# A windowed-attention and MLP kernel: two tensors of the first four chunks loaded in runs of four tokens, and fifty operations with ranks of their own

## The chip, the cores and the metric

The kernel runs on one core of a Trainium2 chip. The time is the device time of one execution in microseconds (us): 217.26 as the median of three runs before the change (217.12 to 218.15). The trace comes from one profiled execution, which took 217.13 us; its span, from the first to the last recorded instruction, is 215.5 us.

The core has TensorE (PE, matmuls; its weight loads are shown apart as PEld), VectorE (DVE), ScalarE (ACT), GpSimd (POOL) and SyncE (SP). SP, ACT and POOL also issue transfers to 16 DMA engines; POOL's transfers can change the type (f32 to bf16) on the way.

## What is computed

Attention over 4 batches, 8 heads, 768 tokens and 64 dimensions, in which a token sees the 4 first tokens and the last 128 up to itself; then a layer norm and an MLP with residual over 512 features:

```python
scores = scale * np.matmul(q, k.transpose(0, 1, 3, 2))
keep = is_sink | in_window
scores = np.where(keep, scores, -1000000000.0)
a = np.exp(scores - np.max(scores, axis=-1, keepdims=True))
a = a / (np.sum(a, axis=-1, keepdims=True) + 1e-09)
attn_out = np.matmul(a, v)
...
x = attn_out.transpose(0, 2, 1, 3).reshape(B, S, H * D)
xn = (x - mu) / np.sqrt(var + 1e-06) * g_ln
out = x + np.maximum(xn @ w_ch1, 0.0) @ w_ch2
```

Inputs and output are float32; the matmuls run in bf16.

## The kernel before

The 3072 tokens are 24 tiles of 128; two tiles make a chunk, three chunks a batch, so there are 12 chunks, each with one MLP of 256 tokens.

For scores the kernel needs q and k with the dimensions on the partitions (kT and qT: four pairs of heads, 128 rows for a pair, 256 tokens). It gets them in three ways. Chunk 0 is loaded in f32 by SP (k) and ACT (q), two loads each for four heads (L666, into natf), cast to bf16 (L670, natc), transposed by matmuls against an identity (L678) and evicted from PSUM into kT and qT (L649). Chunks 1 to 3 are loaded and cast by POOL (L584, into natp), transposed on PE (L597 for chunk 1, one tensor at a time; L604 for chunks 2 and 3, k and q together) and evicted. Chunks 4 to 11 are transposed by the DMA engines. In chunks 0 to 3 a row of the staging tile holds two neighbouring tokens of a head, 512 bytes in the input; the eviction puts the tokens back in order.

Tiles 0 to 3 are attended one by one (`attend_tile`): the mask is added by matmuls (L750) for tiles 0 to 2 and applied on DVE (L780) for tile 3; scores on PE (L770 for tiles 0 and 1, L729 after), exp on ACT (L777), and for tiles 2 and 3 scores against the first four tokens (L785, exp L788). The values (L852, L857) are followed by the reciprocal and the scaling (L870, L872) and by `normalise`: statistics, aggregate and subtraction of the mean on DVE (L880, L882, L884), the power on POOL (L889, L890). For tiles 0 to 3 the result xc is transposed on PE (L897) and evicted with g_ln into xnt (L908). From chunk 2 on the DMA engines do this transpose, and w1 is scaled by g_ln once instead (L1108, L1109), after the MLPs of chunks 0 and 1 have used it unscaled.

The MLP of chunk 0 works by single tiles (L1038), the others by 256 tokens (L1045); relu is on ACT (L1055) or DVE (L1057), the second layer is L1074 and its end L1082. Where PE has a gap in the first 24 us, matmuls on constants fill it (L1146).

Nothing of this is issued in the order of the source. Every step is an operation of a planner (`Plan.op`) with the engines it may run on, a cost, a rank (`prio`, smaller is earlier) and the buffers it needs. `Plan.run` lays them out once, when the program is built, and takes among the operations that could start at about the same time the one of the smallest rank:

```python
t0 = min(c[0] for c in cand[e])
st, o, took = min((c for c in cand[e] if c[0] <= t0 + self.WINDOW[e]), key=lambda c: (c[1].prio, c[1].seq))
```

The result is one fixed list for each engine, carried out in order: an instruction that waits holds up everything behind it on its engine. Costs of transfers are constants such as `SW_P` (L217) and `HW_F` (L219); they decide the order alone. POOL's transfers are served in the order of issue and use eight semaphores in turn, so POOL waits before it issues a ninth until the first has landed.

Of the kernel before, what the change touches and what calls it, by code (L numbers as in the profile page):

```python
# [65 lines left out]
class Plan:  # L66
# [9 lines left out]
    def __init__(self):  # L76
        self.ops = []
        self.rings = {}

# [3 lines left out]
    def op(self, name, engs, prio, emit, reads=(), writes=(), rw=(), dma=None, after=(), mode="n", hold=(), nb=0.0):  # L83
        o = Op()
        o.name, o.engs, o.prio, o.emit, o.dma = name, engs, prio, emit, dma
# [125 lines left out]
def fix(occ, extra=0.09):  # L211
# [5 lines left out]
SW_P = (1.47, 0.7, 0.9)  # L217
SW_W = (2.65, 0.7, 0.9)
HW_F = (0.8, 2.2, 0.5)  # L219
# [13 lines left out]
           w1p=(1.6, 2.6, 2.7, 2.8), pm=3, w2p=(4.5, 4.51, 4.52, 4.53), apart=2, vs0=(2.0, 13.0), by_tile=1, vp=(0.0, 0.1, 2.0, 2.1, 4.55, 4.56), ld1=0.05, t0=0.8, warm=5.6, pm0=-40.0, w1g=17.0, gtt=1.25)  # L233

# [134 lines left out]
def kernel(  # L369
# [42 lines left out]
    ring("natf", 2, [128, H, 2, 64], FP32)  # L412
    ring("natc", 4, [128, 2, 4, 64], BF16)
    ring("nat", 8, [128, H, 64], BF16)
    ring("natp", 4, [128, H, 2, 64], BF16)
    ring("vn", 7, [128, H, 65], BF16)
    ring("kT", 4, [128, HP, 256], BF16)
    ring("qT", 3, [128, HP, 256], BF16)
# [159 lines left out]
    def by_pairs(c, what, d):  # L578
        b, R = c // RC, c % RC
        nats, pts, whole = [], [], len(what) == 1  # L580
        for nm, src, T, ld in what:
            nat = Buf(f"{nm}n{c}", "natp")
            ap = src[b, :, 256 * R:256 * R + 256, :].rearrange("h (p i) d -> p h (i d)", i=2)
            P.op(f"{nm}ld{c}", {"POOL": (0.9, 0.93)}, ld, lambda e, nat=nat, ap=ap: G.dma_start(  # L584
                nat.t.rearrange("p h i d -> p h (i d)"), ap), writes=[nat], dma=SW_P)
            nats.append(nat)
            pts.append([Buf(f"pt{nm}{c}", "pair")] if len(what) > 1 else [Buf(f"pt{nm}{2 * c + r}", "one") for r in range(2)])

        def half(pt, r):
            return (pt[0].t[:, r, :] if len(pt) == 1 else pt[r].t).rearrange("p (h i m) -> p h i m", h=HP, i=2)  # L590

        def tr(e):
            for nat, pt in zip(nats, pts):
                for hp in range(HP):
                    for i in range(2):
                        for h2 in range(2) if whole else ():
                            nc.tensor.matmul(pt[hp // 2].t[64 * h2:64 * h2 + 64, 256 * (hp % 2) + 128 * i:256 * (hp % 2) + 128 * i + 128],  # L597
                                             lhsT=nat.t[:, 2 * hp + h2, i, :], rhs=ident, start=True, stop=True, skip_group_check=True)
                        if whole:
                            continue  # L600
                        for h2 in range(2):
                            for r in range(2):
                                rs, cs = slice(64 * r, 64 * r + 64), slice(64 * h2, 64 * h2 + 64)
                                nc.tensor.matmul(half(pt, r)[cs, hp, i, :], lhsT=nat.t[rs, 2 * hp + h2, i, :],  # L604
                                                 rhs=ident[rs, rs], start=True, stop=True, skip_group_check=True)
        o = P.op(f"tr{what[0][0]}{c}", pe(0.45 if whole else 0.28 * len(what)), d, tr, reads=nats + [Bc["ident"]], hold=[w[2] for w in what],
                 writes=[x for pt in pts for x in pt], mode="h" if whole else "q")
        for (nm, src, T, ld), pt in zip(what, pts):
            for r in range(2):
                t, done = 2 * c + r, Buf(f"{nm}T{2 * c + r}")  # L610
                if c == 1:
                    trs[t] = [o]
                evict(f"ev{nm}{t}", d + 0.05 + 0.02 * r, 512,
                      lambda pt=pt, r=r: pt[r].t.rearrange("p (h i m) -> p h m i", h=2, i=2) if whole else
# [575 lines left out]
```

## Time and profile before

| | us |
|---|---|
| median of three runs | 217.26 |
| the profiled execution | 217.13 |
| its span | 215.5 |
| PE busy | 207.7 |
| DVE, ACT, POOL busy | 114.7, 110.0, 111.4 |
| matmuls of the MLPs: L1074, L1045, L1038 busy | 87.4, 79.3, 8.1 |

The profile shows when each instruction ran and what ended the wait before it. The chain of waits follows the last instruction back to what released it, step by step. A line number stands for the kernel's line, an arrow for what is written from what; buffer numbers are left out. The DMA engines are at 0.9 or more of their time in nearly every slice up to about 160 us.

### The profile page before, as it was taken

The numbers are of one execution on the slowest core, as the hardware profiler recorded it, in microseconds if no ns is written. First come the engines' busy times: TensorE is split into PE (matmuls) and PEld (weight loads), VectorE is DVE, ScalarE is ACT, GpSimd is POOL, SyncE is SP. The second block draws the span as 40 slices with busy tenths as digits, with TensorE's granted clock in tenths as the row PEclk, the third lists the DMA queues.
The fourth block names the chain that finished last, engine by engine and source line by source line (L and its number), as shares of the span: only waits on it lengthen the run. The fifth ranks groups of instructions, "written<-read, shape, count | busy, mean of one in ns | idle before, by whom it ended". The sixth has DMA issues, their size and how long they took to land.

```text
span 215.5 us, 6681 instructions
## 1 busy us (share of the span) xinstructions
PE 207.7 (96%) x2766; PEld 144.2 (67%) x2766; DVE 114.7 (53%) x315; ACT 110.0 (51%) x178; POOL 111.4 (52%) x166
## 2 busy tenths in 40 slices
PE   6799999999999999999999999999999999999992
PEld 2567975755865865865865865865865865866862
DVE  5689875698355356356355356356265365353011
ACT  4796497395662562562652652652652652621600
POOL 7978542499871980971971980971970120110000
PEclk9999999999999999999999999999999999999999
DMA  5999999999999999899899899896899202202102
GB/s 155 189 189 208 191 207 192 185 150 146 167 188 180 110 139 137 90 177 143 117 110 177 117 147 144 109 157 127 117 119 162 75 3 76 73 3 81 41 20 93
DMA packets 104557, 28.07 MB, mean 130 GB/s; under 512 B 94788, under 2 KB 101576, under 8 KB 104520
## 3 DMA queue, kind: packets, MB, share of 16 engines
q0 software_dynamic: 69872, 13.18, 92.2%
q1 hardware_dynamic: 33592, 13.87, 35.2%
q10 hardware_dynamic: 1056, 0.52, 0.9%
q8 instruction: 23, 0.38, 0.8%
q14 instruction: 14, 0.11, 0.2%
HBM read 27.43 MB, written 6.29 MB: 156 GB/s over the span
## 4 chain that ended last, share of the span: by engine, by line
PE 89%; DVE 5%; DMA 2%; ACT 1%; issue 1%; SPq 0%; DVEq 0%
PE one L1074 40%; PE one L1045 36%; PE pair L979 3%; DMA natf<-in_k_dram 2%; PE one L952 2%; PE one L959 2%; PE one L968 1%; DVE st L880 1%; DVE xnt L908 1%; PE one L987 1%; PE one L1038 1%; DVE x L872 1%; PE pair L604 1%; PE pair L729 1%; DVE pe L780 1%
## 5 line engine op out<-in xcount | busy, mean ns | idle before, releaser
L1074 PE MATMUL one<-w,h 128*128 128x512 bf16 (+1 forms) x400 | 87.4, 371 | 0.0
L1055 ACT ACTIVATE h<-one 128x512 bf16<-128x512 f32 x93 | 55.6, 598 | 46.9 <-PE one L1045 42.6
L1045 PE MATMUL one<-xnt,w 128*128 128x256 bf16 x704 | 79.3, 273 | 0.0
L1045 PEld LDWEIGHTS <-w 128*128 128x128 bf16 x704 | 68.6, 98 | 10.4
L1074 PEld LDWEIGHTS <-h 128*128 128x128 bf16 x400 | 37.3, 98 | 39.6
L997 ACT ACTIVATE pe<-pair 128x768 bf16<-128x768 f32 x36 | 27.2, 810 | 41.0 <-PE pair L979 41.0
L644 POOL DMA_DIRECT2D vn<-in_v_dram x59 | 38.7, 694 | 11.4 <-DMA w<-in_moe_w_ch_dram 6.8
L889 POOL TENSOR_SCALAR st<-st 128x1 f32<-128x1 f32 x24 | 8.5, 355 | 61.8 <-DVE st L882 61.2
L1020 DVE RECIPROCAL rec<-one 128x4 f32<-128x4 f32 x36 | 6.4, 178 | 62.9 <-PE one L968 51.4
L1082 DVE SCALAR_TENSOR_TENSOR ot<-one,st,x 128x512 f32<-128x512 f32 (+1 forms) x25 | 18.2, 728 | 13.9 <-PE one L1074 9.0
L890 POOL TENSOR_TENSOR st<-st,mhalf 128x1 f32<-128x1 f32 x24 | 16.7, 696 | 2.0
L880 DVE BATCH_NORM_STATS2 st<-x 128x6 f32<-128x512 bf16 x24 | 16.7, 695 | 0.8
L1022 DVE TENSOR_TENSOR x<-one,rec 128x256 bf16<-128x256 f32 x36 | 15.3, 425 | 1.2
L702 POOL DMA_DIRECT2D nat<-in_k_dram x16 | 15.0, 938 | 1.6 <-DMA natp<-in_q_dram 1.0
L702 POOL DMA_DIRECT2D nat<-in_q_dram x16 | 14.3, 905 | 0.0
L1002 DVE TENSOR_TENSOR pe<-pe,band 128x768 bf16<-128x768 bf16 x24 | 12.2, 551 | 0.0
L979 PE MATMUL pair<-qT,kT 64*64 64x128 bf16 (+1 forms) x528 | 9.2, 204 | 0.0
L884 DVE TENSOR_SCALAR xc<-x,st 128x512 bf16<-128x512 bf16 x24 | 8.5, 353 | 0.9
L952 PEld LDWEIGHTS <-pe 128*128 128x128 bf16 (+1 forms) x144 | 6.2, 97 | 2.9 <-issue 0.8
L1038 PE MATMUL one<-xnt,w 128*128 128x128 bf16 x128 | 8.1, 219 | 0.0
L777 ACT ACTIVATE pe<-pair 128x1024 bf16<-128x1024 f32 (+1 forms) x8 | 7.1, 916 | 1.8 <-PE pair L729 1.4
L979 PEld LDWEIGHTS <-kT 64*64 64x64 bf16 x528 | 7.2, 108 | 0.4 <-ACT w L1109 0.4
(110 smaller groups left out, 165.1 us busy)
## 6 DMA issues: line engine op xcount, KB each, us to landing
out_dram<-ot SPq DMA_DIRECT2D x23, 256.0 KB
w<-in_moe_w_ch_dram POOLq DMA_DIRECT2D x8, 512.0 KB, 14.8
nat<-in_k_dram POOLq DMA_DIRECT2D x16, 128.0 KB, 4.5
nat<-in_q_dram POOLq DMA_DIRECT2D x16, 128.0 KB, 5.3
vn<-in_v_dram POOLq DMA_DIRECT2D x44, 32.0 KB, 5.9
vn<-in_v_dram POOLq DMA_DIRECT2D x15, 64.0 KB, 6.1
natp<-in_k_dram POOLq DMA_DIRECT2D x3, 256.0 KB, 14.7
vn<-in_v_dram POOLq DMA_DIRECT2D x6, 128.0 KB, 9.3
```

The lines of the kernel that those rows point to most:

```text
L644: P.op(f"vld{t}_{i}", {"POOL": (0.8, 0.85)}, prio + 0.001 * i, lambda e, p0=p0, n=n, hs=hs, src=src: G.dma_start(m.t[p0:p0 + n, hs, 0:64], ...
L702: lambda e, nat=nat, ap=ap: G.dma_start(nat.t, ap), writes=[nat], dma=SW, after=gate(c))
L880: P.op(f"bn{t}", {"DVE": fix(0.60)}, d + 0.12, lambda e: V.bn_stats(st.t[:, 8:14], x.t), reads=[x], writes=[st, mv])
L890: G.tensor_tensor(st.t[:, 16:17], st.t[:, 17:18], mhalf, op=ALU.pow)),
L979: nc.tensor.matmul(pps[u].t[64 * g:64 * g + 64, h2, col + c0:col + c0 + n], lhsT=kt.t[rs, hp, k0:k0 + 64], rhs=qT.t[rs, hp, q0:q0 + n], st ...
L997: nc.scalar.activation(pes[j].t.rearrange("p a b -> p (a b)")[:, 0:768].rearrange("p (a b) -> p a b", a=2), pps[j].t[:, :, 0:384], AF.Exp, ...
L1002: V.tensor_mul(at_s, at_s, band[j] if r > 1 else edge[r][j].unsqueeze(1).to_broadcast([128, 4, 192]))
L1022: P.op(f"x{t - 1}{u}", {"DVE": dve(256)}, d + 0.051 + 0.002 * u, lambda e, u=u, rc=rc, pv=pv: V.tensor_tensor(x.t[:, 256 * u:256 * u + 256 ...
L1045: nc.tensor.matmul(ph.t[:, 256 * s:256 * s + 256], lhsT=w1[ht // 4][:, j, 128 * (ht % 4):128 * (ht % 4 + 1)], rhs=xnt.t[:, j, :], start=j ...
L1055: nc.scalar.activation(hb.t, ph.t, AF.Relu)
L1074: nc.tensor.matmul(pc.t[:, 0:wd], lhsT=(h1[2 * s + i].t[:, 128 * ii:128 * ii + 128] if by_tile else h1[ht // 2].t[:, 256 * (ht % 2) + 128 ...
L1082: V.scalar_tensor_tensor(ot.t[:, sl], in0=pc.t[:, 0:wd], scalar=st.t[:, 16:17], in1=x.t[:, sl], op0=ALU.mult, op1=ALU.add),
```

## The change

Chunks 0 to 3 are loaded in runs of four tokens, 1 KB of the input, instead of two. A staging row holds four tokens of a head, and 64 rows hold the 256 tokens of a chunk; the other 64 rows hold other heads (chunks 1 to 3) or the other tensor (chunk 0). Each load of chunks 1 to 3 becomes two, for four heads and 64 partitions each (`by_fours` instead of `by_pairs`). In chunk 0 one staging tile holds k (rows 0 to 63) and q (rows 64 to 127) of the same four heads; each cast and transpose then makes k and q of one pair of heads at once, and kT and qT of chunk 0 lie in one tile `kq0`. The number of transposing matmuls and evictions stays.

A table `NUDGE` adds to the ranks of 50 operations: the new order was found by a search. Two cost constants of the planner follow the new loads. The scaling of w1 waits for the last use of each of its two halves per part instead of the last one in the source's order.

```diff
     def op(self, name, engs, prio, emit, reads=(), writes=(), rw=(), dma=None, after=(), mode="n", hold=(), nb=0.0):
         o = Op()
+        n = self.named[name] = self.named.get(name, -1) + 1
+        prio += NUDGE.get(f"{name}#{n}" if n else name, 0.0)
...
-SW_P = (1.47, 0.7, 0.9)
+SW_P = (0.67, 0.7, 0.9)
...
-HW_F = (0.8, 2.2, 0.5)
+HW_F = (0.7, 2.2, 0.5)
...
+NUDGE = {
+    "ones0": 42.7, "w1ld1": 0.5, "w2ld0": 1.4, "w2ld2": 9.4, "w2ld3": 12.6, "kld0": 12.3, "evf0": 11.2, "cast2": 16.2, "vld0": -14.7,
+    "vld1": -4.6, "x00": 17.1, "x01": 126.8, "ag0": 64.6, "evx0": 9.4, "sc1_0": -11.3, "rc11": -11.1, "trk1": -3, "sc2_0": -89.5,
+    "pm21": -8.8, "bn2": 46.3, "ag2": 5.7, "xc2": 32.2, "trx2": 17.1, "sc3_1": -91, "mk3_1": -6.3, "sk3": -9.1, "x30": 21, "xc3": 78.7,
+    "trx3": 69, "vld4": 5.5, "sc21": -16.1, "xc4": 6.1, "bn5": 21.8, "rs5": 21.5, "kld30": -6.8, "kld31": 11, "qld31": -10.4, "evq7": -6.2,
+    "vld6_0": -13.3, "vld6_1": -3.5, "vld6_3": -1.7, "vld7_0": 33, "vld8_0": -12.1, "vld8_1": -8.7, "vld9_0": 70.9, "vld9_2": -8.9,
+    "kld50": 7.4, "vld10_0": 7.7, "o10": 43.1, "pc40_1": -1.8}
...
-    ring("natf", 2, [128, H, 2, 64], FP32)
-    ring("natc", 4, [128, 2, 4, 64], BF16)
+    ring("natf", 2, [128, 4, 4, 64], FP32)
+    ring("natc", 4, [128, 4, 2, 64], BF16)
...
-    ring("natp", 4, [128, H, 2, 64], BF16)
+    ring("natp", 4, [128, 4, 4, 64], BF16)
...
+    kq0 = consts.tile([128, 2, HP, 256], BF16, name="kq0")
...
-    def by_pairs(c, what, d):
+    def by_fours(c, what, d):
...
-            ap = src[b, :, 256 * R:256 * R + 256, :].rearrange("h (p i) d -> p h (i d)", i=2)
-            P.op(f"{nm}ld{c}", {"POOL": (0.9, 0.93)}, ld, lambda e, nat=nat, ap=ap: G.dma_start(
-                nat.t.rearrange("p h i d -> p h (i d)"), ap), writes=[nat], dma=SW_P)
+            for hh in range(2):
+                ap = src[b, 4 * hh:4 * hh + 4, 256 * R:256 * R + 256, :].rearrange("h (g i) d -> g h (i d)", i=4)
+                P.op(f"{nm}ld{c}{hh}", {"POOL": (0.6, 0.63)}, ld + 0.001 * hh, lambda e, nat=nat, ap=ap, hh=hh: G.dma_start(
+                    nat.t[64 * hh:64 * hh + 64].rearrange("p h i d -> p h (i d)"), ap), writes=[nat], dma=SW_P)
...
+                            for hh in range(2):
+                                rs = slice(64 * hh, 64 * hh + 64)
+                                nc.tensor.matmul(half(pt, hh)[64 * h2:64 * h2 + 64, h1, i, :], lhsT=nat.t[rs, 2 * h1 + h2, i, :],
                                                  rhs=ident[rs, rs], start=True, stop=True, skip_group_check=True)
...
                 for hh in range(2):
-                    hs = slice(4 * hh, 4 * hh + 4)
-                    for i, (x, T) in enumerate(((k, kT_b[c]), (q, qT_b[c]))):
-                        nm, src, part = "kq"[i], nats[i], Buf(f"{'kq'[i]}l{hh}")
-                        ap = x[b, hs, 0:256, :].rearrange("h (p i) d -> p h (i d)", i=2)
+                    src, part, done = Buf(f"f{hh}", "natf"), Buf(f"fl{hh}"), Buf(f"kqT{hh}")
+                    for w, x in enumerate((k, q)):
+                        ap = x[b, 4 * hh:4 * hh + 4, 0:256, :].rearrange("h (g i) d -> g h (i d)", i=4)
+                        P.op(f"{'kq'[w]}ld{hh}", {("SP", "ACT")[w]: (0.53, 0.53)}, -70 + hh,
+                             lambda e, src=src, ap=ap, w=w: (nc.sync if e == "SP" else nc.scalar).dma_start(
+                                 src.t[64 * w:64 * w + 64].rearrange("p h i d -> p h (i d)"), ap), writes=[src, part], dma=HW_F)
+                    for h1 in range(2):
+                        u = 2 * hh + h1
+                        nat, pt = Buf(f"c{u}", "natc"), Buf(f"pt{u}", "one")
+                        P.op(f"cast{u}", {"DVE": dve(512), "ACT": act(512)}, d + 0.01 * u,
+                             lambda e, nat=nat, src=src, h1=h1: (nc.scalar.copy if e == "ACT" else V.tensor_copy)(
+                                 nat.t, src.t[:, 2 * h1:2 * h1 + 2].rearrange("p h i d -> p i h d")),
...
+                        evict(f"evf{u}", d + 0.05 + 0.01 * u, 512,
+                              lambda pt=pt: pt.t.rearrange("p (i w g) -> p w g i", i=4, w=2),
+                              lambda u=u: kq0[:, :, u, :].rearrange("p w (g i) -> p w g i", i=4), [pt], [*T2, done], fp=True)
...
-            last_use[u // 2] = [o]
+            last_use.setdefault(u // 2, []).append(o)
```

In the order that the changed program has, compared with the one before:

- SP issues k of heads 4 to 7 first, then of heads 0 to 3; ACT issues q of heads 0 to 3 first. Two casts of chunk 0 are on ACT and two on DVE (before: four on ACT); so are the four evictions (before: three on DVE, one on ACT).
- On POOL the loads of chunk 1 stand as k, k, q, then two loads of v, then q's other half; the first layer's weights come in the order 0, 2, 3, 1, the second layer's in the order 1, 0, 2, 3, with loads of v, k and q between them.
- On PE the transposes of chunk 1's k stand between the first and the second group of tile 0's scores. The transposes of tile 1's xc and the first values of tile 2 stand ahead of the first MLP matmul (before: behind it). There are 7 matmuls on constants of 256 columns, all ahead of the first transposes (before: 12, all behind them).
- In chunk 1 DVE evicts both halves of k and ACT both of q (before: DVE one of the four, ACT three). DVE runs reciprocals, x, statistics and xc of tiles 0 and 1 before the two evictions into xnt, and likewise for tiles 2 and 3; all eight relus of the first MLP are on ACT.

## The prediction

> **What bounds the kernel now.** I read the head of the page first, then the busy time of each engine in stretches, cut where the chain of waits changes its engine. The columns are: stretch, length, then for PE, PEld, DVE, ACT and POOL the busy time with the count, the granted clock, the DMA share and GB/s.
>
> ```profile
> span 215.5 us, 6681 instructions
> ...
> 5.38:15.37 9.99, 8.69 (x172) 5.58 (x173) 7.45 (x19) 8.04 (x14) 8.24 (x12) 1.00 1.80 189
> 15.37:27.10 11.73, 10.83 (x201) 9.89 (x198) 10.60 (x33) 6.47 (x10) 8.69 (x14) 1.00 1.40 199
> 27.10:211.70 184.60, 184.59 (x2390) 127.51 (x2388) 93.46 (x242) 93.30 (x152) 90.27 (x133) 1.00 1.30 123
> 211.70:215.50 3.80, 0.00 (x0) 0.00 (x0) 0.48 (x1) 0.00 (x0) 0.00 (x0) 1.00 0.25 82
> ```
>
> From 27.10 us to 211.70 us PE is never idle (184.59 of 184.60), and 3.80 us of output follow. At 27.10 the first matmuls of the second MLP start (L1045). The changed program has the same matmuls behind that point, so its time is the moment at which that matmul starts, plus 184.60, plus 3.80, as long as no new wait appears. So the whole question is the first 27.10 us, in which PE also runs matmuls on constants that only fill gaps (L1146):
>
> ```profile
> 5.38:15.37 9.99, 1.83 (x9) 0.67 (x9) 1.00 1.80 189
> 15.37:27.10 11.73, 0.49 (x3) 0.25 (x3) 1.00 1.40 199
> ```
>
> Idle (1.30 and 0.90 us) and fillers (1.83 and 0.49) make 4.5 us that a better start could use; that is the ceiling. The chain of waits (start, length, what) names what sets the pace:
>
> ```profile
> 1.54 4.97 DMA natf<-in_k_dram
> 6.53 0.63 ACT natc L670
> ...
> 9.34 0.51 PE pair L770 x12
> ...
> 11.22 0.33 PE pair L770 x8
> ...
> 14.20 0.69 DVE xnt L908
> ...
> 15.01 0.43 DVE x L872
> 15.47 0.71 DVE st L880
> 16.20 0.19 DVE st L882
> 16.42 0.35 DVE xc L884
> ...
> 20.45 0.60 DVE pe L780
> ...
> 24.50 0.37 DVE xc L884
> ...
> 25.31 1.79 PE one L1038 x32
> 27.10 0.87 PE one L1045 x8
> ...
> 53.68 6.99 PE one L1045 x64
> ```
>
> First the load of chunk 0 (to 6.53), then a hand-to-hand of ACT and PE, and from 14.20 to 24.87 DVE alone: normalisation, masks and the evictions into xnt.
>
> **Chunk 0: the load.** Its four loads carried 2048 packets of 512 B; they become 1024 of 1 KB. The price of a packet comes from windows that hold nearly one kind each: 4 to 5 us (chunk 0, 512 B), 24.5 to 25.5 us (L584: 512 B read, 256 B written), 18 to 20 us (weights: 2 KB read, 1 KB written), 14.5 to 15.5 us (v: 256 B read, 128 B written).
>
> ```profile
> DMA packets 670, 0.33 MB, mean 331 GB/s; under 512 B 24, under 2 KB 670, under 8 KB 670
> ...
> DMA packets 692, 0.18 MB, mean 182 GB/s; under 512 B 682, under 2 KB 692, under 8 KB 692
> ...
> DMA packets 415, 0.42 MB, mean 208 GB/s; under 512 B 9, under 2 KB 415, under 8 KB 415
> ...
> DMA packets 815, 0.19 MB, mean 192 GB/s; under 512 B 732, under 2 KB 814, under 8 KB 814
> ```
>
> Per engine of 16 a packet of the first three starts every 23.9, 23.1 and 77.1 ns. A packet that reads 1 KB lies a third of the way from 512 B to 2 KB: 41 ns (estimate), against 46 to 48 for two of 512 B. Chunk 0 then takes 2.6 us of transfer and not 3.06: 0.4 us less. The bounds are no gain at all (bytes alone count) and half the time (packets alone count, 1.5 us less). I take 0.4, because the three rows lie near a line in bytes.
>
> The landing also changes its meaning. Before, the first cast waits for k of four heads only. Now one staging tile holds k of four heads in rows 0 to 63 and q in rows 64 to 127, and the ranks make SP issue the second half of k first: each tile needs one load that was issued second. The casts lose their early start:
>
> ```profile
> 4.70 1.14 ACT L670 CAST natc<-natf 128x512 bf16<-128x512 f32 x2 [1.05 <-DMA natf<-in_k_dram]
> ...
> 6.53 1.18 ACT L670 CAST natc<-natf 128x512 bf16<-128x512 f32 x2 [0.69 <-DMA natf<-in_k_dram]
> ...
> 7.64 0.69 DVE L649 CAST kT<-one 128x512 bf16<-128x512 f32 x1 [0.54 <-PE one L678]
> ...
> 8.37 0.72 DVE L711 COPY kts<-kT 64x16 bf16<-64x16 bf16 x2
> 8.69 0.60 ACT L777 ACTIVATE pe<-pair 128x512 bf16<-128x512 f32 x1
> ...
> 9.34 0.51 PE L770 MATMUL pair<-qT,kT 64*128 64x128 bf16 x12 [0.48 <-ACT pe L777]
> ```
>
> For q's second half nothing waited. In the window of 2 to 7 us (GB/s in 40 slices of 0.125 us; q10 is ACT's queue: packets, MB, share, and these are all it has)
>
> ```profile
> GB/s 0 94 123 115 106 115 66 53 111 307 336 328 344 369 336 336 344 356 340 328 344 356 291 287 295 287 295 283 291 299 283 277 246 226 189 186 174 190 180 182
> ...
> q10 hardware_dynamic: 1056, 0.52, 39.3%
> ```
>
> it is through by 7.0: I take 6.9 for q and 6.53 for k. Less 0.3 to 0.4 us that is 6.2 and 6.5, so the first cast starts 1.5 us later than 4.70. But four casts now go two by two: ACT takes 0.62 each, DVE has no such row (bounds 0.35, L884's copy in bf16, and 0.69, L649's from PSUM; I take 0.69, which also has f32 input). Casts end at 6.8 and 7.4 on ACT, 6.9 and 7.5 on DVE. The first transposes follow at 6.85; an eviction starts 0.44 us behind its transposes (7.21 to 7.64 above as 7.20 to 7.64: cast end 7.16). So ACT evicts at 7.5 and 8.05, DVE at 7.5 and 8.1, and all of chunk 0 stands at 8.75, where it stood at 8.80 before. The first exp (L777) starts at 8.55 instead of 8.69. The second group of scores waits for that exp's end, as in the row at 9.34 (it writes into the same PSUM tile): 9.2 instead of 9.34. All of this is worth 0.15 us.
>
> **Chunk 1 and the DVE chain.** PE's new order puts the transposes of k's chunk 1 ahead of that second group, inside the wait: the first group of scores runs from 8.1, when DVE's first eviction is done, to 8.3, and then PE reaches them. Their load is now two DMAs of 64 partitions, served behind chunk 0; 512 packets at 41 ns are 1.3 us, so it lands at about 7.9. POOL issues twice as many, at 0.6 us each by L644's loads of 32 KB (256 packets, as many as a half has):
>
> ```profile
> 30.24 0.63 POOL L644 DMA_DIRECT2D vn<-in_v_dram x1 [1.03 <-DMA w<-in_moe_w_ch_dram]
> ...
> 24.82 0.88 POOL L626 DMA_DIRECT2D vn<-in_v_dram x1 [2.13 <-DMA w<-in_moe_w_ch_dram]
> ```
>
> against 0.9 for one of 128 partitions. q's second half stands behind two loads of v (1.0 to 1.25 us each by the window of v) and lands between 11.2 and 11.7; PE gets to it at about 11.7, one value group (0.35) behind the scores of tile 1, which ended at 11.55 and now stand 0.15 earlier. These covers are thin, 0.4 us and less; what it costs without them is the third rival.
>
> DVE now evicts both halves of chunk 1's k (before: one, ACT took the other). From 8.7 it runs kts 0.7, two evictions 0.65 and 0.69, gt 0.16: the first reciprocal comes at 10.9, against
>
> ```profile
> 10.85 0.17 DVE L870 RECIPROCAL rec<-one 128x4 f32<-128x4 f32 x1
> ```
>
> Then the ranks let DVE finish x, statistics and xc of two tiles before it turns to xnt. Per tile that is two reciprocals 0.2, two x 0.44, statistics 0.71, aggregate 0.2, xc 0.35: 2.54 us, for two tiles 5.1. It ends at 16.0; xnt of tile 0 is done at 16.65 (before 14.89) and of tile 1 at 17.3. So MLP 0 starts 1.25 us later than its 15.37, but from then PE has everything it needs.
>
> **The PE sum.** From 16.0 to the matmul at 27.10's place PE has left: eight groups of L1038 at 1.79/2 = 0.9 (7.16), four value groups, scores of tile 3, and three transposes of xc:
>
> ```profile
> 17.06 0.27 PE L852 MATMUL one<-vs,ps 128*128 128x260 bf16 x1
> ...
> 17.41 0.28 PE L852 MATMUL one<-vs,ps 128*128 128x260 bf16 x1
> ...
> 17.86 0.37 PE L729 MATMUL pair<-qT,kT 64*64 64x64 bf16 x16
> 18.16 1.07 PE L1038 MATMUL one<-xnt,w 128*128 128x128 bf16 x16
> ```
>
> Start to start these give 0.35 to 0.45 per value group (1.6), 0.3 for the scores, and 0.25 per transpose (0.75): 9.8, and 0.4 for handovers: 10.2, hence 26.2. DVE must deliver xc of tile 3 by about 24.1: from 17.3 it has two more tiles (5.1), two masks (1.3) and 0.3 waiting for an exp: 24.0. Two chains that end together slip; I add 0.2. So the matmul comes at 26.4 instead of 27.10: **0.7 us less**. The span becomes 214.8; the profiled execution took 217.13 around a span of 215.5 (1.63 outside it), so 216.43, and the median of the runs (217.26) lies 0.13 above that execution: 216.5.
>
> Behind 26.4 I cost nothing: the transposes of chunks 2 and 3 keep their 64 instructions each, and PE's row of 184.60 leaves every other engine at half load or less. The scaling of w1 (L1108, L1109) now waits for both MLPs that use it unscaled; the third MLP, which needs it, began at 53.68 in the chain, long after the second one's last such matmul.
>
> The last weights of the first layer bound the gain: in the row at 24.82 POOL waited for the load of w1's last part, landed by then. Its place in the queue is kept; chunk 0 (0.4) and two loads of chunk 1 (0.16 each) bring it to 24.1, and PE asks for it at 24.6 (two groups of 0.9 ahead of 26.4). So only 0.5 us more could be gained before that load decides, unless packets save more than I take: at half the price landing and weights move by 1.5 us and more, and the end by 1.8 in all (215.4).
>
> The Trainium skill (DMA: Bandwidth & Descriptors, Rules for kernel authors) speaks against the halves: two transfers to disjoint halves of the partitions serialize, one of 128 should be used. Its fit in Anatomy of one DMA gives about 2 us fixed per transfer; paid in turn by the second half, that would put k of chunk 1 at 9.9 and the whole at 218.1, as the third rival counts. The trace rather shows overlap: in the second stretch the DMA share is 1.80, so nearly two packets are in flight on each engine.
>
> **The rivals.**
> (1) *Packets, not bytes, set the start.* The row of GB/s above climbs slowly: about 110 in the first us, 336 after it. If halving the packets doubles the early rate, the landing comes 0.9 to 1.0 us earlier instead of 0.4, all chains shift by 0.6 more, and weights too: 215.9, in the best case 215.4. Against it: the rows above lie on a line in bytes.
> (2) *It does not do what it says.* What the start gains is paid back by MLP 0's late begin: if DVE's list slips by 0.7 (waits between dependent steps that my sum leaves out), PE idles before tile 3's transposes and the second MLP starts at 27.1 again: 217.2.
> (3) *Slower: the transposes of chunk 1's k block PE's queue.* They now stand ahead of the second group of scores; whatever the halves land after 8.3 is added one for one to scores, exp, DVE and end. The price starts to outweigh the 0.7 at a landing of 9.0; if halves on 64 partitions move at half the rate (2.6 us for k), it lands at 9.2, and q's at 13.0 where 11.7 is asked: 1.3 us late; the weights, 2.6 us later than 24.1, stall PE by another 1.0: 216.5 + 2.3 = 218.8. For it: no load on 64 partitions stands alone in the trace. Against: nothing there shows that rows of the target matter.
>
> **How the numbers follow.** My forecast has 0.45, rival 1 0.22, rival 2 0.14, rival 3 0.19. A measurement tells about 0.5% (1.09 us) from no change, so faster means below 216.17. Rival 1 is faster (0.22), and of the forecast's own range, 215.9 to 217.0, a third is (0.14); rival 3 is slower in most of its reach (0.18). Faster 0.36, same 0.46, slower 0.18. The range for 8 in 10 goes from just under rival 1's best case, 215.3, to 218.2, inside rival 3.
>
> **What would show it.** Right: casts on ACT first at about 6.2 and shared with DVE; the exp at 8.55; no filler behind the first transposes; xnt of tile 0 near 16; PE without gap from there; the second MLP's first matmul at 26.4; 184.6 us behind it. Wrong: PE waiting on natp at 8.3 or on w1 before its last two groups; a gap behind 27 us; DVE idle between 11 and 16.

## The result, and the profile after

| | median, us | executions | ratio to before, 95% |
|---|---|---|---|
| before | 217.13 | 216.97 to 218.15 (5) | |
| changed | 221.14 | 218.78 to 222.18 (5) | 1.0129 [1.0089, 1.0169] |

The change made the kernel slower by 1.3%. Ratios, here and below, leave out executions more than 1.5% above the fastest of the same kernel (here 222.18), so they are not the quotients of the medians. The profiled execution was the fastest of the five (218.78 us around a span of 217.3). Three more single executions later took 219.60, 219.97 and 220.10; the median of all eight is 220.0.

The stretches of the trace after, cut at the places that answer to those of before (length, busy time with count of PE, PEld, DVE, ACT, POOL, then granted clock, DMA share, GB/s):

```profile
span 217.3 us, 6649 instructions
...
5.38:15.37 9.99, 6.01 (x71) 4.19 (x68) 4.96 (x13) 4.32 (x7) 7.30 (x11) 0.66 1.63 187
15.37:29.27 13.90, 13.74 (x298) 12.12 (x293) 12.16 (x38) 10.25 (x16) 9.31 (x17) 1.00 1.38 200
29.27:213.95 184.68, 182.41 (x2367) 127.42 (x2388) 93.74 (x246) 91.50 (x149) 92.20 (x136) 1.00 1.23 122
213.95:217.30 3.35, 0.00 (x1) 0.00 (x0) 0.48 (x1) 0.00 (x0) 0.00 (x0) 0.87 0.27 88
```

The body is as long as before (184.68 us against 184.60; the 2.3 us that PE seems idle in it are largely matmuls that the trace lacks, 2367 records against 2390). It starts 2.17 us later. The stretch up to 15.37 holds 6.01 us of PE work instead of 8.69, at a granted clock of 0.66 instead of 1.00. The chain of waits, then ACT's and PE's timelines, show why:

```profile
1.85 7.14 DMA natf<-in_k_dram
...
9.08 0.63 ACT natc L685
...
9.75 1.89 PE one L691 x16
...
27.48 1.79 PE one L1051 x32
29.27 0.87 PE one L1058 x8
```
```profile
9.08 1.14 ACT L685 CAST natc<-natf 128x512 bf16<-128x512 f32 x2 [5.13 <-DMA natf<-in_k_dram]
```
```profile
4.82 0.94 PE L1159 MATMUL one<-const-bfloat16-1.0 128*128 128x256 bf16 x7
9.75 1.89 PE L691 MATMUL one<-ident,natc 128*128 128x128 bf16 x16 [3.98 <-ACT natc L685]
```

The first cast starts at 9.08, where before they stood at 4.70 and 6.53. From the last filler (5.76) to 9.75 PE has nothing to do, its clock is halved, and the 16 first transposes take 1.89 us.

### The profile page after: what moved, and what is told of

It is laid out like the page before. It is cut to its first block, busy times and chain, and to the rows that moved or that the text cites. A ratio compares the mean times of both kernels' runs of the same rounds, so it can differ in the third digit from the quotient of the medians.

```text
span 217.3 us, 6649 instructions
## 1 busy us (share of the span) xinstructions
PE 206.5 (95%) x2738; PEld 145.5 (67%) x2761; DVE 113.7 (52%) x319; ACT 107.6 (50%) x174; POOL 113.0 (52%) x172
## 4 chain that ended last, share of the span: by engine, by line
PE 91%; DMA 5%; issue 1%; ACT 1%; SPq 0%; DVE 0%; DVEq 0%; ACTq 0%
PE one L1087 37%; PE one L1058 36%; PE one L1051 3%; DMA natf<-in_k_dram 3%; PE pair L992 3%; PE one L965 2%; DMA xnt<-xc 2%; PE one L972 2%; PE one L981 1%; PE one L870 1%; PE pair L742 1%; PE one L691 1%; PE one L1000 1%; PE pair L763 1%; PE one L612 1%
## 5 line engine op out<-in xcount | busy, mean ns | idle before, releaser
L1087 PE MATMUL one<-w,h 128*128 128x512 bf16 (+1 forms) x377 | 84.4, 370 | 2.3 <-issue 1.4
L1058 PE MATMUL one<-xnt,w 128*128 128x256 bf16 x704 | 79.3, 273 | 0.0
L1058 PEld LDWEIGHTS <-w 128*128 128x128 bf16 x704 | 68.5, 98 | 10.6 <-DMA xnt<-xc 0.4
L1051 PEld LDWEIGHTS <-w 128*128 128x128 bf16 x128 | 7.2, 98 | 0.1
L965 PE MATMUL one<-vn,pe 128*128 128x65 bf16 (+1 forms) x144 | 7.0, 193 | 0.0
```

The lines of the kernel that those rows point to most:

```text
L965: nc.tensor.matmul(po[h // 4].t[:, 65 * (h % 4):65 * (h % 4) + 65], lhsT=pe_[rs, col:col + 128], rhs=vn_b[t - 1].t[rs, h, :], start=h % 4 ...
L1051: nc.tensor.matmul(ph.t[:, 128 * s:128 * s + 128], lhsT=w1[u // 2][:, j, 128 * s:128 * s + 128], rhs=xnt.t[:, j, 128 * (u % 2):128 * (u % ...
L1058: nc.tensor.matmul(ph.t[:, 256 * s:256 * s + 256], lhsT=w1[ht // 4][:, j, 128 * (ht % 4):128 * (ht % 4 + 1)], rhs=xnt.t[:, j, :], start=j ...
L1087: nc.tensor.matmul(pc.t[:, 0:wd], lhsT=(h1[2 * s + i].t[:, 128 * ii:128 * ii + 128] if by_tile else h1[ht // 2].t[:, 256 * (ht % 2) + 128 ...
```

## Experiments: the opening

Each run's expectation was written before it ran. Ratios are against before on the same chip.

**The order of SP's two loads (k0swap).** SP issued k's second half first and ACT q's first half, so no half was complete until the last load. Here the two are exchanged and nothing else.

```diff
+    i0, i1 = (next(i for i, z in enumerate(items) if z[2].name == n) for n in ("kld0", "kld1"))
+    items[i0], items[i1] = (*items[i1][:2], items[i0][2]), (*items[i0][:2], items[i1][2])
```

> The changed kernel with its two SyncE loads of chunk 0 in the other order (k of heads 0 to 3 first), the order of everything else as it was. Theory 'order': the first casts waited for the second SyncE load, because SyncE began with the half that ScalarE had not begun with. Then the casts of the first half start when that load lands, near 6.3 us instead of 9.08, those of the second half near 9.1; TensorE isn't idle long enough to lose its clock (granted 1.0 from 8.8 to 15.7 us too); the second MLP starts 1 to 2 us earlier than 29.27, near 27.3 to 28.3, and the time is 218.5 to 220.0 where the changed kernel has about 221. Rival 'slow packets': 1 KB packets to 64 partitions are slower in any order, all four loads land after 8 us, first cast near 8.5 to 9, half clock as before, time within 0.5 of the changed kernel's.

221.05 us (219.01 to 223.16), 1.0126 [1.004, 1.0213]. As "order" said, the first casts go to 6.2, and the second half's stay at 9.0. The second MLP starts about 1.1 us earlier than in the changed kernel's first trace (ns, then first and last start of L1058's matmuls):

```profile
L685 ACT CAST natc<-natf x2: 618/618/618, 6.2 to 9.0; 128x512 bf16<-128x512 f32 x2
...
L1058 PE MATMUL one<-xnt,w x704: 270/273/421, 28.0 to 209.3; 128*128 128x256 bf16 x176
```
```profile
L1058 PE MATMUL one<-xnt,w x704: 272/273/283, 29.1 to 206.5; 128*128 128x256 bf16 x176
```

The first fence is k0swap's, the second the changed kernel's. Not all of the 1.1 us is the order's, though. PE's timeline has a wait of 2.25 us for the second half's casts, and PE lost its clock here too, against theory "order". The run both_swaps (below) has the same order of loads and the same first casts at 6.2; its clock stays halved twice as long, and its second MLP starts at 29.0 (PE's busy time, granted clock, DMA share, GB/s; first k0swap, then both_swaps):

```profile
9.50:12.85 3.35, 3.14 (x41) 0.50 2.07 163
```
```profile
9.30:16.00 6.70, 6.20 (x77) 0.50 1.87 173
```

One trace of the changed kernel (after_b, below) also has a halved stretch of 3.35 us, and starts at 28.3. Compared at the same length of the halved stretch, the order is worth about 0.3 us (28.0 against 28.3) or nothing (29.0 against 28.7 to 29.4); the rest of the 1.1 goes with that length. The time didn't fall to the 218.5 to 220.0 of theory "order". The trace is of this kernel's slowest execution (223.16 us); where that one lost is shown below.

**The clock (warm, k0swap_warm).** 24 more matmuls on constants ahead of the first transposes.

```diff
+    first = next(o for o in order if o.name.startswith("trf") or o.name.startswith("trk") or o.name.startswith("trq"))
+    at_, n_, what = max(z for z in items if z[1] < 0 and z[0] < first.start)
+    items.append((at_ + 0.0001, -24, what))
```

> The changed kernel with 24 more 256-column filler matmuls right ahead of the first transposes, so that TensorE is busy until about 8.4 us instead of 5.8; loads and all orders as they were. Theory 'clock': the half clock from 8.83 to 15.65 us is caused by the idle stretch, and costs part of the loss: the granted clock stays 1.0, the 16 first transposes take about 1.0 us instead of 1.89, the first exponential starts near 11.2 instead of 12.15, and the second MLP starts 0.8 to 1.5 us earlier than 29.27; time 219.6 to 220.4. Rival 'landing alone': the first cast still at 9.1, and the chain from it to the second MLP is set by VectorE and the transfers of xnt, so the time stays within 0.4 us of the changed kernel's though the clock is back.

> Both edits: k of heads 0 to 3 first on SyncE, and the 24 fillers. If the order alone already keeps the clock, the fillers end after the first cast (about 8.4 against 6.9 us for the first transposes) and hold the transposes back by up to 1.5 us: time 0.3 to 1.5 us above that of the order alone. If the order alone loses the clock, both together are the best of the four, 217.5 to 219.

The clock stayed at 1.00 through the opening. The second MLP started at 27.8 with the casts still at 9.0; in the four traces of the changed kernel it starts at 28.3 (clock halved for 3.4 us) and at 28.7 to 29.4 (6.8 us). So the halved clock goes with 0.5 to 1.6 us of opening. In warm the load of w1's last part decides in its place, as the chain shows:

```profile
12.36 13.62 DMA w<-in_moe_w_ch_dram
...
26.02 1.96 PE one L1051 x32
27.98 0.87 PE one L1058 x8
```

The times were 221.86 (1.0176 [1.0099, 1.0254]) and, with both edits, 221.31 (1.0166 [1.0089, 1.0244]): no gain, against the 219.6 to 220.4 of theory "clock" and, since the order alone had lost the clock, the 217.5 to 219 expected of both edits. In warm's trace PE waits 2.04 us for a transposed xnt (the normalised tokens, transposed by a DMA), and then runs at half clock again:

```profile
55.73 4.46 PE L1058 MATMUL one<-xnt,w 128*128 128x256 bf16 x24 [2.04 <-DMA xnt<-xc]
```
```profile
56.05:59.40 3.35, 3.35 (x18) 0.50 1.87 206
```

Together that is 3.7 us (2.04, and half of 3.35), more than the opening had won. Another part lies outside the spans (218.6 to 220.4 and 217.5 to 219.4): 1.8 to 3.5 us in these two kernels, 1.4 to 1.7 in all others.

**Sharing with POOL's loads (poolwait).** POOL reads an element of both staging tiles in each row before its first load.

```diff
...
+            if s >= 0 and o.name == "kld10":
+                for i, f in enumerate(f_all):
+                    G.tensor_copy(spare[:, i], f.t[:, 0, 0, 0:1])
```

> The changed kernel, where GpSimd first reads one element of each of the two tiles of chunk 0, so that its loads of chunk 1 and of v start only when all of chunk 0 has landed. Theory 'sharing': the loads of chunk 1, which began at 5.75 us, took the transfer engines from chunk 0's last load; without them the casts start at 7.2 to 7.8 us instead of 9.08, while chunk 1's k lands at 10 or later instead of 8.6. Rival 'slow packets': the casts still start at 8.7 or later. The time itself may go either way, 219 to 222, since chunk 1 then comes later.

226.20 us, 1.0373 [1.0293, 1.0453]. The last load landed at 8.17 (the trace's chain: 1.85 plus 6.32) instead of 8.82 to 8.99 in the traces of the changed kernel: sharing costs 0.7 to 0.8 us, and the casts come between the bounds of the two theories, at 8.25. Even alone, though, the loads land at least 1 us later than before, where the last cast waited for none and started at 7.1. The price of holding POOL back (v and chunk 1 late) is far larger than that. This run shows the loads with nothing beside them. DMA totals and queues of poolwait in the windows 4 to 5 and 5 to 6 us (q1 is SP's queue, q10 ACT's):

```profile
DMA packets 246, 0.24 MB, mean 237 GB/s; under 512 B 15, under 2 KB 246, under 8 KB 246
q1 hardware_dynamic: 199, 0.19, 90.4%
q10 hardware_dynamic: 47, 0.05, 23.2%
...
DMA packets 237, 0.23 MB, mean 231 GB/s; under 512 B 11, under 2 KB 237, under 8 KB 237
q10 hardware_dynamic: 210, 0.21, 99.1%
q1 hardware_dynamic: 27, 0.02, 12.8%
```

Before, the window 4 to 5 had 331 GB/s. Here about 230, and the two queues take turns: mostly SP's packets in one microsecond, mostly ACT's in the next, and from 6 to 7 SP's again (220 of 240 packets, 227 GB/s). The trace of fours0_noranks, in which POOL's packets begin after 6 us, has the same turns, at 257, 234 and 232 GB/s.

**128 partitions instead of 64 (wide, wide_noranks).** The same 1 KB packets, 256 in each load, but two heads over 512 tokens, so that a load fills 128 partitions.

```diff
-                        ap = x[b, 4 * hh:4 * hh + 4, 0:256, :].rearrange("h (g i) d -> g h (i d)", i=4)
+                        ap = x[b, 4 * hh:4 * hh + 2, 0:512, :].rearrange("h (g i) d -> g h (i d)", i=4)
...
-                                 src.t[64 * w:64 * w + 64].rearrange("p h i d -> p h (i d)"), ap), writes=[src, part], dma=HW_F)
+                                 src.t[:, 2 * w:2 * w + 2].rearrange("p h i d -> p h (i d)"), ap), writes=[src, part], dma=HW_F)
```

> The changed kernel, where each of chunk 0's four loads reads two heads over 512 tokens in place of four heads over 256: the same 256 packets of 1 KB, but to 128 partitions each instead of 64 (the attention of chunk 0 is then computed on the wrong tokens). Theory '64 partitions': packets of 1 KB to 64 partitions took about 79 ns at 5 to 7 us; to 128 partitions they take 45 to 55, the first casts start at 7.0 to 7.8 instead of 9.1. Rival '1 KB packets': still 75 ns or more each and the casts at 8.7 or later.

wide, 4 to 5 us, its casts, and the start of its second MLP in the chain of waits:

```profile
DMA packets 404, 0.38 MB, mean 381 GB/s; under 512 B 32, under 2 KB 404, under 8 KB 404
```
```profile
L685 DVE CAST natc<-natf x2: 408/448/487, 5.5 to 5.9; 128x512 bf16<-128x512 f32 x2
L685 ACT CAST natc<-natf x2: 617/618/619, 6.5 to 7.1; 128x512 bf16<-128x512 f32 x2
...
L1058 PE MATMUL one<-xnt,w x704: 269/273/421, 26.3 to 208.5; 128*128 128x256 bf16 x176
```
```profile
26.45 0.87 PE one L1058 x8
```

Packets of the same size move at 381 GB/s, casts start at 5.5 and 6.5, and the second MLP at 26.45 in the chain, level with the forecast's 26.4 and 0.65 ahead of before (27.10). So it is the load to 64 rows that costs, and the earlier start that was forecast is there without it. (The loads of wide also read two heads of 512 tokens instead of four of 256; that this plays no part was not tested apart.) The Trainium skill has a cause for it (SBUF — State Buffer, Door 1: The DMA port swizzle): partitions 0 to 63 reach 8 of the 16 ports, for about 218 GB/s. The rows of 227 to 237 lie 4 to 9% above that; each of these windows also holds packets of the other queue, to the other 64 rows. Another rule of the Trainium skill, that transfers to disjoint halves serialize (DMA: Bandwidth & Descriptors, Rules for kernel authors), agrees with the queues that take turns.

Still wide took 221.23 us (two executions; 1.0162 [1.0109, 1.0214]). What took the gain back is the order, as the same kernel without ranks shows:

> The wide loads of chunk 0 with an empty table of ranks (planner's order). Theory: the late landing was the whole of the layout's loss, so with loads that land by 7 us the kernel is at 216 to 217.5, no waits for xnt. Rival 'the layout loses elsewhere too' (casts, evictions that carry k and q together, half-width transposes): 218.5 or more.

217.18 us (216.37 to 218.07), 0.9978 [0.9949, 1.0006]: the theory held. It is level with before, in its start too (26.9), and 3.6 us below the same kernel with 64-partition loads (noranks, next).

## Experiments: layout and ranks apart

**noranks** is the changed kernel with an empty table of ranks; **before_ranks** the kernel before with the table (without `kld0`, and without the entries whose operation it lacks); **pairs0** the changed kernel with chunk 0 as before; **pairs0_noranks** and **fours0_noranks** have one half of the layout each; **headranks** drops the 21 entries from `vld4` on.

```diff
-NUDGE = {
...
+NUDGE = {}
```

> The changed kernel with the table of ranks empty: the new layout and its loads, in the order that the planner gives by itself. Theory 'layout': chunk 0's four loads of 1 KB packets to 64 partitions still land late (the last near 8.2 to 9.1 us, where before had 7.1), the second MLP starts at 28 or later, and the time is 218.5 to 220.5. Theory 'ranks': the loss lies in the order found by search, which gave the first tile that goes through a transposing DMA less time before its use; without the ranks the time is 216.8 to 218.2.

> The kernel before, with the table of ranks alone (where the operation exists there, and without the rank of the first k load): runs of two tokens as before. Theory 'layout': within 0.7 us of before (217.0). Theory 'ranks': 218.5 to 220, with waits for xnt of 1 to 2 us in the executions above 218.

> The changed kernel with chunk 0 loaded, cast and transposed as before (512-byte runs of two tokens over 128 partitions, k and q apart), k of heads 0 to 3 first on SyncE; chunks 1 to 3 in runs of four and the ranks stay (where a name still exists). Theory 'layout of chunk 0': the four loads land by 7.1 to 7.6 us, TensorE keeps its clock, the second MLP starts at 27.0 to 27.6, and the time is 217 to 218.5, the rest of the loss being the ranks' waits for xnt. Rival 'chunk 1 and the ranks': the start stays at 28.5 or later, 220 to 222.

> The kernel before with one part of the change: chunks 1 to 3 come in runs of four tokens (1 KB), chunk 0 in runs of two as before, no ranks, planner's order. Theory 'chunk 0': the layout of the later chunks costs nothing, 216.5 to 217.5, second MLP as early as before. Rival 'halves on 64 partitions': chunk 1's loads and half-width transposes cost too, 218.5 or more.

> The other half of the layout: chunk 0 in runs of four, chunks 1 to 3 in runs of two as before, no ranks, planner's order. Theory 'chunk 0': the last of the four loads lands between 8.2 and 9.1 us, TensorE loses its clock for some 7 us, and the time is 219.5 to 221, like both layouts together without ranks (220.82). Rival: below 218, the loss comes from the later chunks.

> The changed kernel with only the 29 ranks of the opening (chunks 0 and 1 and the weights); the 21 ranks of later operations (from the load of v's tile 4 on) are gone. The start of the second MLP stays near 29.3. Theory 'ranks': the later ranks cut the time between the first transposing DMAs of xnt and their use, so that the executions above 219 (the median of the changed kernel is 221) come from waits for xnt of 1 to 2 us; without them the median falls to 218.8 to 219.6. Rival: the waits come from the late opening itself, the median stays at 220.5 to 222.

| chunk 0 | chunks 1 to 3 | ranks | median, us | ratio to before, 95% | second MLP starts, us |
|---|---|---|---|---|---|
| fours, 64 rows | fours | none (noranks) | 220.82 | 1.0165 [1.0116, 1.0213] | 30.9 |
| fours, 64 rows | pairs | none (fours0_noranks) | 220.11 | 1.0104 [1.0040, 1.0168] | 29.9 |
| pairs | fours | none (pairs0_noranks) | 217.99 | 1.0013 [0.9983, 1.0042] | 26.7 |
| fours, 128 rows | fours | none (wide_noranks) | 217.18 | 0.9978 [0.9949, 1.0006] | 26.9 |
| pairs | pairs | yes (before_ranks) | 220.69 | 1.0170 [1.0118, 1.0222] | 31.2 |
| pairs | fours | yes (pairs0) | 219.75 | 1.0096 [1.0059, 1.0132] | 28.2 |
| fours, 128 rows | fours | yes (wide) | 221.23 | 1.0162 [1.0109, 1.0214] | 26.3 |
| fours, 64 rows | fours | first 29 (headranks) | 220.74 | 1.0134 [1.0082, 1.0185] | 29.3 |

The last column is the first start of the second MLP's matmuls in the one trace of each; before has 26.9 there, the changed kernel 28.3 to 29.4.

Three readings. Without ranks the layout's loss is chunk 0's load alone: runs of four in chunks 1 to 3 cost nothing and bring nothing, and the start of the second MLP moves with chunk 0's load. The ranks cost 1 to 2% by themselves where the loads land early (before_ranks, pairs0, and wide against wide_noranks); theory "layout" had expected before_ranks at 217, and was wrong. And the two don't add up: with the late loads the kernel is as slow without ranks (1.0165) as with them (1.0129). The theory of headranks (218.8 to 219.6) missed as well, and pairs0 lies between its theory's 218.5 and its rival's 220. before_ranks has a limit: the table was searched for the other layout, and a part of its entries has no operation there.

How the ranks lose it differs. In before_ranks it is the opening, 4.3 us longer than before's: DVE finishes the statistics of two tiles before it makes xnt, so that PE gets 80 matmuls of the first MLP in one piece and waits ahead of it and behind (1.8 of the 4.3):

```profile
22.89 0.88 PE L909 MATMUL one<-ident,xc 128*128 128x128 bf16 x8 [0.19 <-DVE xc L896]
24.74 4.64 PE L1050 MATMUL one<-xnt,w 128*128 128x128 bf16 x80 [0.98 <-DVE xnt L920]
...
31.21 1.05 PE L1057 MATMUL one<-xnt,w 128*128 128x256 bf16 x8 [0.86 <-DVE xnt L920]
```

In wide and k0swap, whose opening is early, it is a wait far behind it. wide, PE's timeline and the stretches around that wait (busy time of PE, granted clock, DMA share, GB/s):

```profile
72.39 1.94 PE L1058 MATMUL one<-xnt,w 128*128 128x256 bf16 x14 [2.51 <-DMA xnt<-xc]
```
```profile
72.39:73.75 1.36, 1.36 (x13) 0.97 0.60 133
73.75:77.10 3.35, 3.35 (x17) 0.50 1.62 140
77.10:80.00 2.90, 2.90 (x28) 1.00 1.98 202
```

2.51 us of waiting, and 1.35 us after work has resumed the clock halves for 3.35 us: another 1.7. That is 4.2, all that the early start had won and more. k0swap, in its execution of 223.16 us, waits 2.0 us at the same place, and its clock halves behind it too:

```profile
69.42 3.62 DMA xnt<-xc
73.03 0.14 issue
73.17 6.85 PE one L1058 x46
```

pairs0 waits 2.60 us there (in an execution of 222.35 us), and warm 2.04 us for an earlier tile. The traces of the changed kernel, headranks and noranks, which start between 28.3 and 30.9, wait for no more than 0.2; but an early start is not the only way to such a wait, since poolwait, with a start of 33.8, has one of 2.67. SP's queue tells where wide's comes from, wide above, before below:

```profile
57.44 1.25 SPq L589 DMA_TRANSPOSE kT<-nat  x1
58.78 1.26 SPq L589 DMA_TRANSPOSE xnt<-xc  x1
66.81 1.19 SPq L589 DMA_TRANSPOSE kT<-nat  x1
68.09 1.22 SPq L589 DMA_TRANSPOSE xnt<-xc  x1
```
```profile
55.65 1.22 SPq L576 DMA_TRANSPOSE xnt<-xc  x1
...
59.00 2.50 SPq L576 DMA_TRANSPOSE kT<-nat  x2
63.93 1.19 SPq L576 DMA_TRANSPOSE xnt<-xc  x1
```

The ranks split chunk 5's two transposes of kT and put the second (its load has `kld50`, rank +7.4) ahead of xnt's tile 7. xc of that tile was ready at 65.6 (DVE's timeline), but SP stood at kT until 68.0; xnt landed 4.16 us behind its issue.

**Exchanging the two (sp_swap, wide_sp_swap, both_swaps).** The transfer of xnt's tile 7 takes the place of that kT, and kT its. In the program that place lies ahead of the step that writes the tile's xc, so the transfer reads what lay there before and doesn't wait for xc; in return that step has to wait until the transfer has read. So none of the three computes the right output, both_swaps neither, though its expectation calls its results right.

```diff
+    for a, b in [('trk50', 'trx7')]:
+        i0, i1 = (next(i for i, z in enumerate(items) if z[2].name == n) for n in (a, b))
+        items[i0], items[i1] = (*items[i1][:2], items[i0][2]), (*items[i0][:2], items[i1][2])
```

> The changed kernel with one exchange on SyncE: the transposing transfer of xnt's tile 7 goes ahead of the second one of chunk 5's kT, which stood ahead of it and waited for k's load until 67.2 us (where the kernel before issued xnt's at 63.93, ahead of it). Theory 'queue on SyncE': in the variants whose PE waited 2 to 2.6 us for xnt near 70 us the cause was this place; the changed kernel's median falls from 221.1 to 219 to 220, its lowest (218.8, which did not wait) stays. Rival: the spread has another cause, the median stays at 220.5 to 222.

> The wide loads of chunk 0 (256 packets of 1 KB to 128 partitions each; chunk 0's attention on the wrong tokens) with the same exchange on SyncE. The second MLP starts near 26.3 as in the wide run. Theory 'queue on SyncE': the wait for xnt of 2.5 us, with the half clock behind it, goes; 216.0 to 218.0 instead of 221.2. Rival: another xnt transfer is next (the first pair landed at 52.48 and was used at 52.52), 218.5 to 220.5.

> The changed kernel, right results, with both exchanges on SyncE: k of heads 0 to 3 first, and xnt's tile 7 ahead of chunk 5's second kT. Theory: the second MLP starts near 28.0 as with the first exchange alone, and the wait for xnt that took that gain back (2.0 us near 71 us) is gone: 217.8 to 219.3, against 221.05 for the first exchange alone. Rival: 220 or more, the wait moves to another xnt transfer.

wide_sp_swap took 219.66 (1.0114 [1.0057, 1.0171]), 1.6 below wide, though the two intervals overlap. Its trace waits 0.4 for xnt instead of 2.5, keeps its clock, and its last matmul ends at 212.6 instead of 216.0: the place is right for wide's wait. But 219.66 is in the rival's range, and 2.5 us remain above wide_noranks; the runs don't say where these come from. sp_swap took 221.35 (1.0187 [1.0132, 1.0242]) and both_swaps 221.17 (1.0155 [1.0110, 1.0200]): no gain, against the theory (both_swaps exchanges SP's first two loads as well). These two bring a wait of their own, as sp_swap's DVE and PE show:

```profile
70.40 0.35 DVE L897 TENSOR_SCALAR xc<-x,st 128x512 bf16<-128x512 bf16 x1 [2.65 <-DMA xnt<-xc]
```
```profile
71.28 0.20 PE L965 MATMUL one<-vn,pe 128*128 128x65 bf16 x1 [0.78 <-DVE pe L1015]
```

The early transfer was issued at 62.2 and landed only at 70.3; until then DVE could not write xc. So the exchange alone does not tell what the place costs in the changed kernel. In the executions of the changed kernel that were traced it does not set the time: none of the four waits at it, and headranks, without `kld50`, is no faster.

**The changed kernel again (after_again, after_b, after_c).**

> The changed kernel itself, profiled a second time: its first profile was its fastest execution (218.78, median 221.14). Theory 'waits for xnt': in an execution near 221 TensorE waits 1 to 2.6 us for a transposing DMA of xnt between 45 and 80 us, as in three of the variants, and starts the second MLP near 29.3 as in the first profile. Rival 'opening': the extra time lies ahead of the second MLP, which then starts above 30.5.

> The changed kernel a third time, to see the trace of an execution near its median. If it takes 220.5 or more: theory 'waits for xnt', TensorE waits 1 us or more for a transposing transfer of xnt between 45 and 80 us, with a stretch of half clock behind it, and the second MLP starts near 29.3; rival 'opening', the second MLP starts above 30.5; rival 'end', the transfers behind TensorE's last matmul take 1 us more than the 3.4 of the first profile. If it takes less than 219.7 it shows none of these.

> The changed kernel a fourth time, for the same purpose: at 220.5 or more its trace shows a wait for xnt between 45 and 80 us, a later opening, or a longer end, and tells which; below 219.7 it tells nothing new.

They took 219.60, 220.10 and 219.97 us, so none of them shows an execution of 220.5 or more. None waits for xnt for more than 0.2 us. after_b and after_c differ at the end: their last matmuls end at 213.86 and 213.65, no later than in the first trace (213.95), and the span ends 4.7 and 4.8 us behind, not 3.35. after_b:

```profile
span 218.6 us, 6649 instructions
```
```profile
213.59 0.27 PE L1087 MATMUL one<-w,h 128*128 128x256 bf16 x1
213.97 0.48 DVE L1095 SCALAR_TENSOR_TENSOR ot<-one,st,x 128x256 f32<-128x256 f32 x1 [0.73 <-PE one L1087]
```

So 1.4 us of the spread is a later end behind the last store, the rival "end". In after_b small packets of SP's queue still run at 217.0, in the first trace none after 216; the trace names no cause. headranks, k0swap and wide_sp_swap have an end of 4.7 to 4.8 us too. Of the 2.9 us between the median of all eight executions (220.0) and before's, the later start is 1.4 to 2.5 us (28.3 to 29.4 against 26.9), and this end up to 1 us more (4.8 against before's 3.8). Executions of the changed kernel above 221 were never traced; what they lose stays open.

## Why the prediction was wrong, step by step

- **"Chunk 0: the load" is the step that failed.** It took 41 ns a packet and casts at 6.2 and 6.5, between bounds of "no gain at all" and 1.5 us less; a loss was not within the bounds. The casts came at 9.08, 2.6 to 2.9 us later. All rows from which the price was interpolated were of loads to 128 partitions; these go to 64, at about 230 GB/s, and the same packets to 128 rows brought the start to the forecast's (26.45 in wide). Rival 3 had the mechanism ("halves on 64 partitions move at half the rate") and applied it to chunk 1, where it costs nothing, and not to chunk 0, the first link of the chain. Its total of 218.8 meets the first execution by accident. The rule on halves that the prediction quotes from the Trainium skill was dismissed because the DMA share of 1.80 seemed to show overlap: that share came from loads of full height.
- **The granted clock was taken as 1.00 throughout**, as in before. The late landing left PE idle for 4 us, and the halved clock made it 0.5 to 1.6 us dearer (against warm). No term of the sum had it.
- "Each tile needs one load that was issued second" was right: in k0swap the first casts go to 6.2. But it is worth no more than about 0.3 us of opening, compared at the same length of the halved stretch.
- Two by two casts: right, and DVE is quicker than the 0.69 taken (1.16 for two).
- The DVE chain and the PE sum held in size: from the first reciprocal to xnt 4.7 us (14.62 to 19.32; taken 5.1), from tile 1's transposes to the second MLP 9.8 (19.48 to 29.27; taken 10.2 from 16.0). They only began 3.5 to 3.7 us late.
- w1's last part was to land at 24.1; in warm it decided at 25.98.
- "Behind 26.4 I cost nothing" held in the four traces of the changed kernel. In wide, which starts as forecast, the ranks' order of SP's queue took 4.2 us back. This second fault was hidden by the first: with the landing that was forecast the kernel is slower than before all the same (wide, 1.0162). The forecast looked at the moved operations of the first 27 us only, and not at those of SP behind them.

A version faster than before was not found. wide_noranks is level with it and computes chunk 0 on other tokens; a right kernel with such loads would have to bring chunks 0 and 1 together, which was not tried.

## What to carry to other kernels

Price a load by its destination rows as well as by its packets: halves of the partitions ran at about 230 GB/s where full height ran at 381, and two halves on two queues took turns. When the first load of a chain is changed, ask what PE's clock does while it waits; fillers that last until the data is there kept it (warm), though the time of these two kernels did not fall. And an order found for one set of landing times is no gain by itself: test ranks and layout apart, since here each cost 1 to 2% by itself and hid the other.

## What the runs showed of the hardware

- The clock halved 2.5 us after PE's last filler, and came back 5.3 us after the transposes began (changed kernel, first trace); three stretches of the changed kernel (PE's busy time, granted clock, DMA share, GB/s):

```profile
6.00:8.00 2.00, 0.00 (x0) 1.00 1.25 218
8.00:15.00 7.00, 5.25 (x59) 0.51 1.74 178
15.00:18.00 3.00, 3.00 (x65) 0.99 1.72 188
```

Gaps of 1.96 (k0swap), 2.04 (warm) and 2.51 us (wide) were enough, one of 0.88 (k0swap_warm) was not; the halving came when PE was at work again, 0.3 to 1.35 us after it resumed. The Trainium skill (TensorE: Matmul & The Clock Gate, Part 1: The HAM clock gate) has the clock drop after an idle window of about 3.4 us and return after a busy one of about 3.4 us. The length of the halved stretch in wide, 3.35, agrees with the second; the gaps that set it off were shorter than the first.
- Loads by POOL of 64 partitions, which read 1 KB and write 512 B a packet, cost the kernel nothing against full height (pairs0_noranks, 1.0013); only the f32 loads of chunk 0 did.
- 48 more instructions on PE's list (warm) went with 1.8 to 3.5 us outside the span instead of 1.4 to 1.7, without a cause that the traces show.
